# Query groups cut by batch: half tiles of one batch in a group, and all later query products in 32x32 tiles of one length

## The chip, the cores and the metric

The kernel runs on one core of a Trainium2 chip. The metric is the device time of one execution in microseconds (us). A measurement is the median over several executions, and smaller is better.

## What is computed

The reference takes q, k and v of 4 batches, 4 heads, 1088 positions and 32 numbers a head, and two 8x32 sketch matrices S1 and S2. It has an attention part and a feed-forward part:

```
phi(x) = outer product of S1 x and S2 x        (8 x 8 = 64 features for each position)
kv     = sum over positions of phi(k) v^T      (64 x 32 for each batch and head)
z      = sum over positions of phi(k)          (64 for each batch and head)
x      = phi(q) kv / (phi(q) z + 1e-6)         (4352 tokens of 4 heads x 32 = 128)
out    = elu(x w_in) w_out                     (128 -> 2048 -> 128)
```

All arithmetic in the kernel is fp32. Most of the work is the feed-forward part.

## The kernel before

**Half tiles, groups, units.** The 1088 positions of a batch are cut into NT = 17 half tiles of 64 positions, t = 0 to 16; four batches have 68. A group is eight half tiles, 512 tokens; groups 0 to 7 are full, and group 8, the last, has four half tiles. `half_tile(g, k)` (L498) says which batch and which t the k-th half tile of group g is. Before the change it counts straight through, so groups 2, 4 and 6 begin with the last half tiles of one batch (1, 2 and 3 of them) and go on with the next batch. For the query products, groups 4 and 5 are one unit, and so are 6 and 7; groups 2, 3 and 8 are units of their own (`units`, L545; `un[g]` is half the count of half tiles, so 4 for groups 2 and 3, 8 for the pairs and 2 for the last).

**Steps.** The feed-forward part goes through the 2048 hidden columns in eight slices `cp` of 256. One step is one group and one slice. For each step TensorE makes h = x w_in into two PSUM banks (`mm1`, L257), ScalarE and VectorE make elu of it (`e` at L867 and L869, `gg` at L875), and two steps later TensorE multiplies by w_out: as `o` (`mm2`, L257) for group 0, as `pb` (L768) for the first slices of group 1, and by seven products into `pa` and `pb` (L792) for the rest. The latter need sums `tt` of `gg` that GpSimd makes (L751 to L756). The list `steps` writes out the order by hand: 64 steps, the first ones alternating between groups 0 and 1, later ones group by group. The four half tiles of the last group follow in a tail of their own.

**The order of the rest.** All engines run their instructions in the order of the program. What belongs to the attention part is hung by hand on steps: `at(n, f)` puts f after the h products of step n, `mid` after the first half of elu, `late` after the second half.

**Keys.** For batches 1 to 3, `KF_late`, `KO`, `KA`, `Z`, `KV` make the features of the keys, kv and z. `KV_out` (L462) copies kv out of PSUM. It writes `kvs[b]`, one 32x32 block for each head, for 32x32 products, and `kvq[b]`, which has two heads in a block of 64 with zeros elsewhere (a VectorE multiplication by `cmask`), for 64x64 products. In the same way `Z_share` (L452) writes `SWq`, the sketches and z of two heads apart, and `SWs`, their sum over the two, the weights for 32x32 products.

**Queries.** `queries(g5, g1, n+1)` (L704) is hung on steps 13, 15, 22, 30, 46 and 62. It issues the products q5 of unit g5 (features of q times kv, L686; two halves f, which accumulate) and the products q1 of unit g1 (sketches of q and the denominator, L576). At step 13 there is only q1 of unit 2, at 15 q5 of 2 and q1 of 3, at 22 q5 of 3 and q1 of 4, at 30 q5 of 4 and q1 of 6, at 46 q5 of 6 and q1 of 8, at 62 only q5 of 8.

Units 2, 3 and 8 are `wide_tiles`: their products are 64x64 tiles of the array (four tiles) and write two banks of the pool `aux`. Units 4 and 6 use 32x32 tiles (sixteen tiles) and write four banks, two of `aux` and two of the pool `h`. Those two are the banks of the next step's h, taken early. That pool has four banks, two for each of two steps running.

Each tile of the array has its own run of half tiles. Where that run crosses from one batch to the next, `parts` (L558) splits it, and the product is made in pieces. All first pieces are issued, then the second ones (the sort by `j` at L572 and L681).

After the products VectorE transposes q1's result out of PSUM (`q1_out`, L589, tile `abw`), makes the denominator, its reciprocal and the features (`q2_den`, `q2_half`) and transposes these (`q4`, tile `qpT`). ScalarE copies q5's result into `xg`, the input of the h products (`q5_out`, L699 and L701).

The tile `qT[b]` has the transposed queries of one batch; batches 0 and 2 share one, and so do 1 and 3. Batch 2 is written over batch 0 at step 21, batch 3 over batch 1 late in step 24.

Of the kernel before, what the change touches and what calls it, by code (L numbers as in the profile page):

```python
# [27 lines left out]
def kernel(  # L28
# [44 lines left out]
    qT = [const.tile([FD, NT, 64], F32, name=f"qT{b}") for b in range(2)] * 2  # L73

# [168 lines left out]
    cmask = const.tile([P, 2], F32, name="cmask")  # L243
    nc.gpsimd.tensor_add(cmask[:], bmask[:, :2], bmask[:, 2:])
# [52 lines left out]
    SWq = const.tile([FD, B, 2, 4, R], F32, name="SWq")  # L297
    SWs = const.tile([FD, B - 1, 4, R], F32, name="SWs")
# [16 lines left out]
    def make_SWq():  # L315
        nc.gpsimd.memset(SWq[:, :, :, 3, :].rearrange("p b c r -> p (b c) r"), 0.0)
        for b in range(B):
            nc.gpsimd.tensor_copy(SWq[:, b, :, :2, :].rearrange("p c x r -> p x c r"), Sxp[:])
# [10 lines left out]
    kvq = {b: const.tile([P, 2, H, D], F32, name=f"kvq{b}") for b in (0, 1, 3)}  # L329
    kvs = {b: const.tile([P, 2, H, D], F32, name=f"kvs{b}") for b in (1, 2, 3)}  # L330
# [121 lines left out]
    def Z_share(b):  # L452
        z = wzs.pop(b)
        nc.gpsimd.tensor_add(SWq[:, b, :, 2, :], z[:, :2], z[:, 2:])
        if b:
            nc.gpsimd.tensor_add(SWs[:, b - 1], SWq[:, b, 0], SWq[:, b, 1])
# [5 lines left out]
    def KV_out(b, ps):  # L462
        if b in kvs:
            copy = nc.scalar.copy if b in kvq else nc.vector.tensor_copy
            copy(kvs[b][:].rearrange("p f h d -> p (f h d)"), ps[:, 128:384])
        if b in kvq:
            nc.vector.tensor_mul(kvq[b][:].rearrange("p f (g c) d -> p (f g) c d", c=2),
                                 ps[:, 128:384].rearrange("p (x c d) -> p x c d", c=2, d=D),
                                 _ap(cmask[:], [[0, 4], [1, 2], [0, D]]))
# [27 lines left out]

    def half_tile(g, k):  # L498
        return divmod(8 * g + k, NT)

    def runs(g):

        h = 0
        while h < 2 * qn[g]:
            b, t = divmod(8 * g + h, NT)
            m = min(2 * qn[g] - h, NT - t)
            yield b, t, h, m
            h += m
# [38 lines left out]

    def wide_tiles(g):
        return un[g] < 8

    def parts(g, w):  # L558

        n = un[g] if wide_tiles(g) else un[g] // 2  # L560
        k = 0
        while k < n:
            b, t = half_tile(g, n * w + k)
            m = min(n - k, NT - t)
            yield b, t, k, m
            k += m

    def q1(g, ps, o, opened):
        s = 64 if wide_tiles(g) else 32
        n = P // s  # L570
        todo = [(j, w, r, x) for w in range(n) for r in range(n) for j, x in enumerate(parts(g, w))]
        for j, w, r, (b, t, k, m) in sorted(todo, key=lambda x: x[0]):  # L572
            rows = slice(s * r, s * r + s)
            lhs = SWq[rows, b].rearrange("p c x r -> p (c x r)") if s > 32 else \
                SWs[rows, b - 1].rearrange("p x r -> p (x r)")
            nc.tensor.matmul(ps[r][s * w:s * w + s, o + 64 * k:o + 64 * (k + m)], lhs,  # L576
                             qT[b][rows, t:t + m, :].rearrange("p t s -> p (t s)"),
                             start=j == 0 and not any(ps[r] is x for x in opened), stop=True,
                             skip_group_check=True, tile_position=(s * r, s * w))
        abw[g] = ps, o  # L580
# [95 lines left out]
    def q5(g, ps, f):  # L676
        s = 64 if wide_tiles(g) else 32
        n = P // s
        m4 = H * un[g] // n
        todo = [(j, w, r, x) for r in range(n) for w in range(n) for j, x in enumerate(parts(g, w))]  # L680
        for j, w, r, (b, t, k, m) in sorted(todo, key=lambda x: x[0]):  # L681
            i, o = divmod(m4 * r, heads(g) * un[g])
            rows = slice(s * w, s * w + s)
            lhs = kvq[b][rows, f, 2 * r:2 * r + 2, :].rearrange("p c d -> p (c d)") if s > 32 else \
                kvs[b][rows, f, r, :]
            nc.tensor.matmul(ps[w][s * r:s * r + s, 64 * k:64 * (k + m)], lhs,  # L686
                             qpT[g, i][rows, o + 2 * k:o + 2 * (k + m), f, :],
                             start=(f == 0 and j == 0), stop=(f == 1),
                             skip_group_check=True, tile_position=(s * w, s * r))
        xps[g] = ps  # L690

    def q5_out(g, i=0):

        ps = xps[g]
        n = H * un[g] * 32 // len(ps)
        x = xg[g + i] = work.tile([P, 512], F32, name="xg", tag="xg", bufs=3)
        for w in range(2):
            if g < NQ - 1:
                nc.scalar.copy(x[:, n * w:n * w + n], ps[2 * i + w][:, :n])  # L699
            else:  # L700
                nc.scalar.copy(x[:, :2 * n].rearrange("p (k w s) -> p w k s", w=2, s=64)[:, w],  # L701
                               ps[w][:, :n].rearrange("p (k s) -> p k s", s=64))

    def queries(g5, g1, n):  # L704

        banks = lambda g: 0 if g is None else 2 if wide_tiles(g) else 4
        if banks(g5) + banks(g1) > 4:
            hs[steps[n]] = [psum.tile([P, 512], F32, name="h", tag="h", bufs=4) for c in range(2)]
        aux = [psum.tile([P, 512], F32, name="qps", tag="aux") for _ in range(2)]
        ps = {2: aux, 4: hs.get(steps[n], []) + aux}  # L710
        same = banks(g5) == banks(g1)
        if g5 is not None:
            q5(g5, ps[banks(g5)], 0)
            if not same:
                q5(g5, ps[banks(g5)], 1)
        if g1 is not None:
            q1(g1, ps[banks(g1)], 256 if g5 is not None else 0, ps[banks(g5)] if g5 is not None else [])
        if g5 is not None and same:
            q5(g5, ps[banks(g5)], 1)
# [100 lines left out]
    def fin_seven_b(g):  # L820
# [13 lines left out]
        for u in range(2):  # L834
            k = 0
            while k < 4:
                bt, t = half_tile(g, 4 * u + k)
                m = min(4 - k, NT - t)
                for lo in range(2):
                    r = slice(64 * u + 32 * lo, 64 * u + 32 * lo + 32)  # L840
                    for hi in range(2):
                        for w in range(2):
                            nc.sync.dma_start(rows[bt, w, hi, lo, :, t:t + m, :], ob[r, hi, k:k + m, w, :])
                k += m
# [46 lines left out]
    def fin1(g):  # L891
# [6 lines left out]
        for b, t, h, m in runs(g):  # L898
            for w in range(2):
                for q_ in range(4):  # L900
                    nc.sync.dma_start(rows[b, w, q_, :, t:t + m, :], oh[32 * q_:32 * q_ + 32, h:h + m, w, :])
# [301 lines left out]
```

## Time and profile before

| what | value |
|---|---|
| median of 3 runs | 265.75 us (265.56 to 265.98) |
| span of the profiled execution, first to last instruction | 263.3 us |
| what lies around the span, if that execution took the median | 2.45 us |
| TensorE busy | 257.8 us, 4127 matmul records |
| VectorE, ScalarE, GpSimd busy | 188.2, 184.5, 168.2 us |
| clock granted to TensorE | 1.000 |

The profile is of one execution, which has no time of its own in the table other than its span. Lines L... are lines of the kernel before. Every fp32 matmul leaves two records, and so does every load of weights (PEld). In a timeline row the columns are start, time from the first start to the last end, engine, line, operation, tiles, array tile or shape, and count of records; a bracket names the idle time before the row and what ended it. Times of one engine's rows overlap by the depth of its pipeline, so starts are better compared than ends.

### The profile page before, as it was taken

Reading aid. Unit: us, or ns where it says so; the run is one execution under the profiler, and the core shown is the slowest. Engines: PE = TensorE matmul, PEld = TensorE weight load, DVE = VectorE, ACT = ScalarE, POOL = GpSimd, SP = SyncE. Lnnn points to the kernel's source line nnn. Section 1 sums busy time; section 2 is a strip of 40 time slices with the busy share of each in tenths; the row PEclk is TensorE's granted clock in tenths of the full one; section 3 lists DMA queues with packets and bytes.
Section 4 is the critical chain, followed back from the end, with each engine's and each line's share of the span. In section 5 each row is a group of like instructions: output and inputs, shape, how many; then the busy total and the mean of one; then the engine's idle time right before and its main releaser. Section 6 shows DMA issues by size and latency. Waiting matters only on the chain.

```text
span 263.3 us, 9739 instructions
## 1 busy us (share of the span) xinstructions
PE 257.8 (98%) x4127; PEld 160.5 (61%) x4127; DVE 188.2 (71%) x349; ACT 184.5 (70%) x356; POOL 168.2 (64%) x251
## 2 busy tenths in 40 slices
PE   8899999999999999999999999999999999999994
PEld 7652334354346756667666666665666666667994
DVE  6899999997969997996477676644446445674651
ACT  2479978677567656775587777776777777777793
POOL 4400009105477996798869799888688888998300
PEclk9999999999999999999999999999999999999999
DMA  5997099020011110000100110011001100110011
GB/s 176 339 349 209 2 277 230 1 72 18 2 24 26 26 20 2 2 4 17 31 3 0 29 18 0 2 19 25 3 2 21 23 4 0 18 20 8 2 30 32
DMA packets 26442, 13.73 MB, mean 52 GB/s; under 512 B 19328, under 2 KB 24576, under 8 KB 26400
## 3 DMA queue, kind: packets, MB, share of 16 engines
q1 hardware_dynamic: 25968, 12.76, 18.9%
q8 instruction: 32, 0.52, 0.9%
q10 hardware_dynamic: 368, 0.30, 0.3%
q0 software_dynamic: 64, 0.07, 0.1%
q14 instruction: 10, 0.08, 0.1%
HBM read 10.88 MB, written 2.23 MB: 50 GB/s over the span
## 4 chain that ended last, share of the span: by engine, by line
PE 96%; POOL 1%; DVE 1%; ACT 1%; issue 0%
PE h L257 44%; PE pb L792 16%; PE pa L792 13%; PE o L257 5%; PE pb L768 4%; PE ol L257 3%; PE idle L265 1%; PE kv L428 1%; PE h L686 1%; PE qps L686 1%; POOL kp L324 1%; PE kfps L360 1%; PE qps L576 1%; PE qtp L636 1%; PE kv L257 1%; PE abp L341 1%
## 5 line engine op out<-in xcount | busy, mean ns | idle before, releaser
L257 PE MATMUL h<-xg,W 128*32 128x512 f32 (+3 forms) x904 | 130.7, 539 | 0.4 <-ACT xg L649 0.4
L875 DVE SCALAR_TENSOR_TENSOR gg<-e,h 128x512 f32<-128x512 f32 x128 | 85.6, 683 | 54.1 <-ACT e L869 50.6
L867 ACT ACTIVATE e<-h 128x512 f32<-128x512 f32 x128 | 75.5, 590 | 45.6 <-PE h L257 42.9
L869 ACT ACTIVATE e<-e 128x512 f32<-128x512 f32 x128 | 80.9, 632 | 3.8
L257 PEld LDWEIGHTS h<-xg,W 128*32 128x32 f32 (+1 forms) x904 | 42.6, 122 | 43.2 <-issue 34.9
L754 POOL TENSOR_TENSOR tt<-gg 128x256 f32<-128x256 f32 x50 | 37.0, 741 | 16.4 <-DVE gg L875 16.1
L751 POOL TENSOR_TENSOR tt<-gg 128x256 f32<-128x256 f32 x50 | 36.7, 734 | 5.5 <-DVE gg L875 5.1
L755 POOL TENSOR_TENSOR tt<-tt,gg 128x256 f32<-128x256 f32 x50 | 37.5, 750 | 3.9
L756 POOL TENSOR_TENSOR tt<-gg,tt 128x256 f32<-128x256 f32 x50 | 37.2, 744 | 3.9
L792 PEld LDWEIGHTS pa<-gg,W 128*64 128x64 f32 (+1 forms) x496 | 23.8, 125 | 23.5 <-issue 22.9
L792 PE MATMUL pa<-gg,W 128*64 128x128 f32 (+1 forms) x496 | 30.5, 274 | 0.0
L792 PE MATMUL pb<-tt,SS 128*64 128x128 f32 (+1 forms) x480 | 29.5, 273 | 0.0
L792 PEld LDWEIGHTS pb<-tt,SS 128*64 128x64 f32 (+1 forms) x480 | 22.6, 126 | 0.0
L792 PE MATMUL pa<-tt,SS 128*32 128x128 f32 (+1 forms) x288 | 21.0, 273 | 0.0
L133 POOL TENSOR_TENSOR raw<-raw,tiny 128x512 f32<-128x512 f32 x1 | 1.0, 1044 | 29.4 <-DVE raw L128 29.4
L792 PE MATMUL pb<-tt,W 128*64 128x128 f32 (+1 forms) x256 | 19.8, 273 | 0.0
L792 PE MATMUL pb<-gg,SS 128*64 128x128 f32 (+1 forms) x256 | 19.8, 273 | 0.0
L257 PE MATMUL o<-gg,W 128*32 128x512 f32 x128 | 15.3, 594 | 0.0
L792 PEld LDWEIGHTS pa<-tt,SS 128*32 128x32 f32 (+1 forms) x288 | 13.6, 124 | 0.0
L792 PEld LDWEIGHTS pb<-gg,SS 128*64 128x64 f32 (+1 forms) x256 | 12.7, 125 | 0.0
L792 PEld LDWEIGHTS pb<-tt,W 128*64 128x64 f32 (+1 forms) x256 | 12.6, 125 | 0.0
L768 PE MATMUL pb<-gg,W 128*32 128x256 f32 x192 | 11.5, 380 | 0.0
(163 smaller groups left out, 279.5 us busy)
## 6 DMA issues: line engine op xcount, KB each, us to landing
raw<-in_moe_w_in_dram SPq DMA_DIRECT2D x8, 256.0 KB, 6.6
raw<-in_moe_w_out_dram SPq DMA_DIRECT2D x8, 256.0 KB, 6.4
hd_k<-in_k_dram SPq DMA_DIRECT2D x3, 544.0 KB, 7.3
hd_q<-in_q_dram SPq DMA_DIRECT2D x3, 544.0 KB, 7.9
out_dram<-ob SPq DMA_DIRECT2D x88, 16.0 KB, 1.5
v<-in_v_dram SPq DMA_DIRECT2D x4, 288.0 KB, 6.8
v<-in_v_dram SPq DMA_DIRECT2D x4, 256.0 KB, 8.3
hd_k<-in_k_dram SPq DMA_DIRECT2D x1, 288.0 KB, 3.3
```

The lines of the kernel that those rows point to most:

```text
L257: nc.tensor.matmul(dst[c:c + tile], lhs[:, c:c + tile], rhs, skip_group_check=True, tile_position=(0, c), **kw)
L265: nc.tensor.matmul(idle[c:c + tile, :cols], ones[:, :tile], ones[:, :cols], skip_group_check=True, tile_position=(0, c))
L686: nc.tensor.matmul(ps[w][s * r:s * r + s, 64 * k:64 * (k + m)], lhs, qpT[g, i][rows, o + 2 * k:o + 2 * (k + m), f, :], start=(f == 0 and j ...
L751: nc.gpsimd.tensor_tensor(t[:, 0], b12, b11, op=SUB)
L754: nc.gpsimd.tensor_tensor(t[:, 2], b22, b12, op=SUB)
L755: nc.gpsimd.tensor_tensor(t[:, 1], t[:, 2], b11, op=ADD)
L756: nc.gpsimd.tensor_tensor(t[:, 3], b21, t[:, 1], op=SUB)
L768: nc.tensor.matmul(acc[1][0][r:r + width[0], 256 * hi:256 * hi + 256], lhs[:, w:w + width[0]], gg[:, c, 256 * u:256 * u + 256], start=(cp ...
L792: nc.tensor.matmul(bank[r:r + width[0], P * col:P * col + P], lhs[:, w:w + width[0]], rhs[:, u], start=(first and i in ((0,) if g == 1 els ...
L867: nc.scalar.activation(e, hs[g, cp][c][:, :n], RELU, scale=-1.0)
L869: nc.scalar.activation(e, e, EXP, scale=-1.0)
L875: nc.vector.scalar_tensor_tensor(gs[g, cp][:, c, :n], es[g, cp][:, c, :n], -1.0, hs[g, cp][c][:, :n], op0=ADD, op1=MAX)
```

## The change

Groups now hold half tiles of one batch: group g has the half tiles 8(g mod 2) to 8(g mod 2)+7 of batch g//2, and the last group has half tile 16 of each batch. `parts` and `runs` are gone, since nothing crosses a batch; `quarter_of` gives each of the four row or column strips of the array one run of n half tiles of one batch.

All units from 2 on use 32x32 tiles and four banks, so `queries` always takes the two h banks of the next step, and always in the order q5 first half, q1, q5 second half. `kvq`, `SWq` and `cmask` are gone; `kvs` and `SWs` exist for all batches, `SWs` made by GpSimd in `make_SWs` and `Z_share`. `q1_out` and `q5_out` empty four banks instead of two for units 2, 3 and 8, each operation half as wide. `qE` keeps half tile 16 of batches 0 and 1, copied by GpSimd at steps 3 and 14 (`keep_last`), because `qT` is written over before the last group needs it. The output transfers of groups 2, 4 and 6 are no longer split at a batch (24 fewer).

```diff
+    qE = const.tile([FD, 2, 64], F32, name="qE")
...
-    def make_SWq():
-        nc.gpsimd.memset(SWq[:, :, :, 3, :].rearrange("p b c r -> p (b c) r"), 0.0)
+    def make_SWs():
+        nc.gpsimd.memset(SWs[:, :, 3, :], 0.0)
         for b in range(B):
-            nc.gpsimd.tensor_copy(SWq[:, b, :, :2, :].rearrange("p c x r -> p x c r"), Sxp[:])
+            nc.gpsimd.tensor_add(SWs[:, b, :2, :], Sxp[:, :, 0, :], Sxp[:, :, 1, :])
...
     def Z_share(b):
         z = wzs.pop(b)
-        nc.gpsimd.tensor_add(SWq[:, b, :, 2, :], z[:, :2], z[:, 2:])
-        if b:
-            nc.gpsimd.tensor_add(SWs[:, b - 1], SWq[:, b, 0], SWq[:, b, 1])
+        zh = work.tile([FD, 2, R], F32, name="zh", tag="zh")
+        nc.gpsimd.tensor_add(zh[:], z[:, :2], z[:, 2:])
+        nc.gpsimd.tensor_add(SWs[:, b, 2, :], zh[:, 0], zh[:, 1])
...
     def KV_out(b, ps):
-        if b in kvs:
-            copy = nc.scalar.copy if b in kvq else nc.vector.tensor_copy
-            copy(kvs[b][:].rearrange("p f h d -> p (f h d)"), ps[:, 128:384])
-        if b in kvq:
-            nc.vector.tensor_mul(kvq[b][:].rearrange("p f (g c) d -> p (f g) c d", c=2),
-                                 ps[:, 128:384].rearrange("p (x c d) -> p x c d", c=2, d=D),
-                                 _ap(cmask[:], [[0, 4], [1, 2], [0, D]]))
+        copy = nc.scalar.copy if b % 2 else nc.vector.tensor_copy
+        copy(kvs[b][:].rearrange("p f h d -> p (f h d)"), ps[:, 128:384])
...
+    def keep_last(b):
+        nc.gpsimd.tensor_copy(qE[:, b, :], qT[b][:, NT - 1, :])
+
     def half_tile(g, k):
-        return divmod(8 * g + k, NT)
+        return (g // 2, 8 * (g % 2) + k) if g < NQ - 1 else (k, NT - 1)
...
+    def quarter_of(g, w):
+        n = un[g] // 2
+        return (*half_tile(g + n * w // 8, n * w % 8), n)

     def q1(g, ps, o, opened):
-        s = 64 if wide_tiles(g) else 32
-        n = P // s
-        todo = [(j, w, r, x) for w in range(n) for r in range(n) for j, x in enumerate(parts(g, w))]
...
+        for w in range(4):
+            b, t, n = quarter_of(g, w)
+            qs = qE[:, b:b + 1, :] if g == NQ - 1 and b < 2 else qT[b][:, t:t + n, :]
+            for r in range(4):
+                rows = slice(32 * r, 32 * r + 32)
+                nc.tensor.matmul(ps[r][32 * w:32 * w + 32, o:o + 64 * n], SWs[rows, b].rearrange("p x r -> p (x r)"),
+                                 qs[rows].rearrange("p t s -> p (t s)"),
+                                 start=not opened, stop=True, skip_group_check=True, tile_position=(32 * r, 32 * w))
...
     def q5(g, ps, f):
...
+        m4 = un[g]
+        for r in range(4):
             i, o = divmod(m4 * r, heads(g) * un[g])
...
+            for w in range(4):
+                b, t, n = quarter_of(g, w)
+                rows = slice(32 * w, 32 * w + 32)
+                nc.tensor.matmul(ps[w][32 * r:32 * r + 32, :64 * n], kvs[b][rows, f, r, :],
+                                 qpT[g, i][rows, o:o + 2 * n, f, :], start=(f == 0), stop=(f == 1),
+                                 skip_group_check=True, tile_position=(32 * w, 32 * r))
...
     def q5_out(g, i=0):
-        ps = xps[g]
-        n = H * un[g] * 32 // len(ps)
+        n = 32 * un[g]
+        ps = xps[g] if len(units[g]) == 1 else xps[g][2 * i:2 * i + 2]
...
+        for w in range(len(ps)):
+            nc.scalar.copy(x[:, n * w:n * w + n], ps[w][:, :n])

     def queries(g5, g1, n):
-        banks = lambda g: 0 if g is None else 2 if wide_tiles(g) else 4
-        if banks(g5) + banks(g1) > 4:
-            hs[steps[n]] = [psum.tile([P, 512], F32, name="h", tag="h", bufs=4) for c in range(2)]
-        aux = [psum.tile([P, 512], F32, name="qps", tag="aux") for _ in range(2)]
-        ps = {2: aux, 4: hs.get(steps[n], []) + aux}
-        same = banks(g5) == banks(g1)
+        hs[steps[n]] = [psum.tile([P, 512], F32, name="h", tag="h", bufs=4) for c in range(2)]
+        ps = hs[steps[n]] + [psum.tile([P, 512], F32, name="qps", tag="aux") for _ in range(2)]
         if g5 is not None:
-            q5(g5, ps[banks(g5)], 0)
-            if not same:
-                q5(g5, ps[banks(g5)], 1)
+            q5(g5, ps, 0)
         if g1 is not None:
-            q1(g1, ps[banks(g1)], 256 if g5 is not None else 0, ps[banks(g5)] if g5 is not None else [])
-        if g5 is not None and same:
-            q5(g5, ps[banks(g5)], 1)
+            q1(g1, ps, 256 if g5 is not None else 0, g5 is not None)
+        if g5 is not None:
+            q5(g5, ps, 1)
...
-            b, t = half_tile(NQ - 1, u * qn[NQ - 1] + i)
+            b, t = half_tile(NQ - 1, 2 * i + u)
...
     late(2, make_Sxp)
-    late(2, make_SWq)
+    late(3, keep_last, 0)
+    late(14, keep_last, 1)
+    late(2, make_SWs)
```

More of the change, by code (lines that the diff above doesn't have):

```diff
@@ L240 @@
                             ident[:].rearrange("p (x j) -> p x j", j=R), axis=AX, op=ADD)
-    cmask = const.tile([P, 2], F32, name="cmask")
-    nc.gpsimd.tensor_add(cmask[:], bmask[:, :2], bmask[:, 2:])
     hmask = const.tile([P, H], F32, name="hmask")
@@ L296 @@
     SW = const.tile([FD, H, 3, R], F32, name="SW")
-    SWq = const.tile([FD, B, 2, 4, R], F32, name="SWq")
-    SWs = const.tile([FD, B - 1, 4, R], F32, name="SWs")
+    SWs = const.tile([FD, B, 4, R], F32, name="SWs")
     keep_warm(3)
@@ L328 @@
     kvS = const.tile([P, H, D], F32, name="kvS")
-    kvq = {b: const.tile([P, 2, H, D], F32, name=f"kvq{b}") for b in (0, 1, 3)}
-    kvs = {b: const.tile([P, 2, H, D], F32, name=f"kvs{b}") for b in (1, 2, 3)}
+    kvs = {b: const.tile([P, 2, H, D], F32, name=f"kvs{b}") for b in range(B)}
     kv_ps, kvz, feats, wzs, kf_ps = {}, {}, {}, {}, []
@@ L496 @@
         nc.gpsimd.memset(pw[:, :, R:], 1e-6)
+    def keep_last(b):
+        nc.gpsimd.tensor_copy(qE[:, b, :], qT[b][:, NT - 1, :])
     def half_tile(g, k):
-        return divmod(8 * g + k, NT)
[L501 to L508, printed above, removed]
+        return (g // 2, 8 * (g % 2) + k) if g < NQ - 1 else (k, NT - 1)
     def q1_first():
@@ L546 @@
     un = {g: sum(qn[x] for x in gr) for g, gr in units.items()}
[L555 to L566, printed above, removed]
-    def q1(g, ps, o, opened):
-        s = 64 if wide_tiles(g) else 32
-        n = P // s
-        todo = [(j, w, r, x) for w in range(n) for r in range(n) for j, x in enumerate(parts(g, w))]
[L572 to L579, printed above, removed]
+    def quarter_of(g, w):
+        n = un[g] // 2
+        return (*half_tile(g + n * w // 8, n * w % 8), n)
+    def q1(g, ps, o, opened):
+        for w in range(4):
[6 more added lines that the diff above has]
+                                 start=not opened, stop=True, skip_group_check=True, tile_position=(32 * r, 32 * w))
         abw[g] = ps, o
@@ L676, in q5 @@
     def q5(g, ps, f):
[L677 to L681, printed above, removed]
-            i, o = divmod(m4 * r, heads(g) * un[g])
[L683 to L689, printed above, removed]
+        m4 = un[g]
@@ L692, in q5_out @@
     def q5_out(g, i=0):
-        ps = xps[g]
-        n = H * un[g] * 32 // len(ps)
+        n = 32 * un[g]
+        ps = xps[g] if len(units[g]) == 1 else xps[g][2 * i:2 * i + 2]
         x = xg[g + i] = work.tile([P, 512], F32, name="xg", tag="xg", bufs=3)
[L697 to L702, printed above, removed]
@@ L834, in fin_seven_b @@
         for u in range(2):
[L835 to L844, printed above, removed]
+            bt, t = half_tile(g, 4 * u)
+            for lo in range(2):
+                r = slice(64 * u + 32 * lo, 64 * u + 32 * lo + 32)
+                for hi in range(2):
+                    for w in range(2):
+                        nc.sync.dma_start(rows[bt, w, hi, lo, :, t:t + 4, :], ob[r, hi, :, w, :])
     def mm1(g, cp, cs=(0, 1)):
@@ L897, in fin1 @@
         oh = ob[:].rearrange("p i u w d -> p (i u) w d")
[L898 to L901, printed above, removed]
+        b, t = half_tile(g, 0)
+        for w in range(2):
+            for q_ in range(4):
+                nc.sync.dma_start(rows[b, w, q_, :, t:t + 8, :], oh[32 * q_:32 * q_ + 32, :, w, :])
     last = [(i, cp) for i in range(2) for cp in range(NP)]
```

## The prediction

> **What bounds the kernel now.** I read the busy times and the chain that ended last on the page first, then TensorE's timeline around the six places where query products run, then VectorE's timeline ahead of the second of them.
>
> ```profile
> PE 257.8 (98%) x4127; PEld 160.5 (61%) x4127; DVE 188.2 (71%) x349; ACT 184.5 (70%) x356; POOL 168.2 (64%) x251
> PE 96%; POOL 1%; DVE 1%; ACT 1%; issue 0%
> ```
>
> The chain is TensorE for 96% of the span, so time taken out of TensorE's queue comes off the end unless another engine is late there. A full product h takes 1.72 us from start to next start (67.70 to 69.42 below). The query products are the rows L576 (q1) and L686 (q5).
>
> ```profile
> 61.77 1.94 PE L257 MATMUL h<-xg,W 128*32 128x512 f32 x16
> 63.64 0.66 PE L576 MATMUL qps<-qT,SWq 64*64 64x64 f32 x12
> 64.23 1.93 PE L768 MATMUL pb<-gg,W 128*32 128x256 f32 x32
> ...
> 67.70 1.90 PE L257 MATMUL o<-gg,W 128*32 128x512 f32 x16
> 69.42 1.90 PE L257 MATMUL h<-xg,W 128*32 128x512 f32 x16
> 71.25 0.67 PE L686 MATMUL qps<-qpT,kvq 64*64 64x64 f32 x12
> ...
> 72.72 1.92 PE L257 MATMUL o<-gg,W 128*32 128x512 f32 x16
> ```
>
> Columns: start, time, engine, line, operation, tile, count of records (each fp32 matmul leaves two). From the first query record to the next full product, the six stretches take 0.59 us (step 13: 63.64 to 64.23), 1.47 (step 15: 71.25 to 72.72), 1.94 (step 22: 99.03 to 100.97), 2.40 (step 30: 128.77 to 131.17), 1.97 (step 46: 183.24 to 185.21) and 0.60 (step 62: 237.28 to 237.88): 8.97 us. About 0.1 us of idle ahead of each (71.25 against 69.42+1.72) stays, since the tile shape still changes there. TensorE meets no queue but its own, so these 8.97 us are what the change can touch.
>
> What a 32x32 product costs, and what a split piece costs:
>
> ```profile
> 100.17 0.30 PE L576 MATMUL h<-qT,SWs 32*32 32x128 f32 x2
> ...
> 100.27 0.41 PE L576 MATMUL qps<-qT,SWs 32*32 32x256 f32 x2
> 100.31 0.27 PE L576 MATMUL h<-qT,SWs 32*32 32x128 f32 x2
> ...
> 100.44 0.38 PE L576 MATMUL h<-qT,SWs 32*32 32x256 f32 x2
> ...
> 100.97 0.64 PE L792 MATMUL pa<-gg,W 128*32 128x128 f32 x16
> ```
>
> Sixteen 32x32 products start within 0.107 us (6.7 ns apart) when they come after a change of shape. A tile's second pass starts 0.24 us after its first for 256 columns and 0.133 for 128, where the stream alone is 0.216 and 0.108 (the steady start-to-start of 256-column passes in the 64x64 stretch is 0.216). So one product holds its tile 0.456 us at 256 columns, 0.24 at 128 and, by the same step, about 0.13 at 64.
>
> ```profile
> 183.61 0.73 PE L686 MATMUL h<-qpT,kvs 32*32 32x64 f32 x8
> ...
> 184.03 0.41 PE L686 MATMUL qps<-qpT,kvs 32*32 32x256 f32 x2
> 184.06 0.41 PE L686 MATMUL h<-qpT,kvs 32*32 32x192 f32 x2
> 184.09 0.41 PE L686 MATMUL qps<-qpT,kvs 32*32 32x256 f32 x2
> ...
> 184.83 0.45 PE L576 MATMUL qps<-qT,SWq 64*64 64x128 f32 x8
> ```
>
> Two things are seen. The four leftover 64-column pieces all fall on one row of tiles and stretch from 183.61 to past 183.9, while the other twelve tiles have nothing. And products that follow other 32x32 products start 16.7 ns apart (two to each of the last three rows, and these 0.033 us apart), not 6.7.
>
> **The change part by part.** The listing of both programs has 240 query matmuls after against 162 before, all 32x32, no leftover pieces, three passes in the order q5 first half, q1, q5 second half. I lay them out with 6.7 ns starts for the first sixteen, 16.7 ns for the rest, the tile times above and 0.09 us to the next full product (at step 22 the last pass starts at 100.77, streams 0.108, and the next product starts at 100.97).
> - Step 13, 16 of 128 columns: 0.107+0.24+0.09 = 0.44; gain 0.15.
> - Step 15, 48 of 128: last group starts 0.25 after the last start of the second, which is 0.24+0.25; 0.24+0.25+0.017+0.25+0.24+0.09 = 1.09; gain 0.38.
> - Step 22, 16 of 128, 16 of 256, 16 of 128: 0.24+0.456+0.25+0.24+0.09 = 1.28, and 0.10 for a wait that stays (the second 64x64 record waits there from 99.03 to 99.154 for the bank that VectorE leaves at 99.10): 1.38; gain 0.56. The change of shape between q5(3) and q1(4), 0.09, is in this.
> - Step 30, 48 of 256: 3 x 0.456+0.25+0.09 = 1.71; gain 0.69.
> - Step 46, 16 of 256, 16 of 64, 16 of 256: 0.456+0.267+0.25+0.456+0.09 = 1.52; gain 0.45.
> - Step 62, 32 of 64: 0.107+0.267+0.14+0.09 = 0.60; gain 0.
> Sum 2.23 us. If all groups started 6.7 ns apart, each stretch would be the sum of its tile times and 0.10+0.09 (and the 0.10 of step 22): 0.44, 0.91, 1.23, 1.56, 1.23 and 0.45, gain 3.15. That is the other end; the steady rows are at 16.7, so I stay near the first.
>
> The change also adds a wait. Steps 13, 15 and 62 (and q5 at 22) now write two banks of the pool h, which the step before must have left: its second gg on VectorE must be done.
>
> ```profile
> 69.28 1.24 DVE L673 STREAM_TRANSPOSE qpT<-qp 128x1024 f32<-128x1024 f32 x1
> 70.45 0.65 DVE L875 SCALAR_TENSOR_TENSOR gg<-e,h 128x512 f32<-128x512 f32 x1
> 71.02 1.29 DVE L281 STREAM_TRANSPOSE kT<-hd_k 128x1088 f32<-128x1088 f32 x1
> ```
>
> At step 15 that gg ends at 71.10, after a VectorE chain without a gap since 64.20, and four 128x128 transposes stand in that chain where two of 128x256 did. The two took 0.70 us start to start; 128x128 ones at step 46 took 0.32 and 0.27, 0.24 and 0.20 without the overlap, so four take 0.84: +0.14. The bank is free at 71.24, seen by TensorE 0.05 later (99.10 to 99.154), while TensorE is ready at 71.25-0.15 = 71.10: a new wait of 0.19. Behind it in TensorE's queue stand q1(3), the second half of q5(2) and the o product, all of which end later by it. At step 13 the gg before ends at 62.11 against 63.64, at step 62 at 236.42 against 237.28: nothing.
>
> Afterwards the next h product must wait until copies and transposes leave its two banks. The hardest place is step 30, already so before: transposes end at 132.46, h starts at 132.74. Elsewhere the operations are half as wide; ScalarE has about 0.1 us more (four copies of 128x128: the two at step 62 start 0.16 apart; two of 128x256 take 0.53) and stands idle 1.1 and 1.6 us before them at steps 15 and 22; at step 62 it has 0.2, but the sums made of that step are read 2.1 us after they are ready, 242.75 to 244.89. I take nothing.
>
> Costed at nothing: three VectorE multiplications for kvq (0.42 us each) go and one copy (0.41) comes, in a queue that then waits 1.1 us for ScalarE at step 13; GpSimd gets two copies of 128x64 (a 128x32 copy takes 0.21), one in a 1.25 us hole at 74.2, and its sums are ready 1.2 us or more before TensorE reads them at the tightest step (t3 of step 23 ends at 110.84, read at 112.04), so a step that came 1.2 us closer would show it; 24 output transfers fewer leave SP's queue, which nothing waits for. The end of the kernel has the same instructions.
>
> Sum: 2.23-0.19 = 2.04 us; 3.15-0.19 = 2.96 at the other end. I take 2.15. The profiled execution has a span of 263.3 us, 2.45 below the median of 265.75; I keep that rest, so 265.75-2.15 = 263.6, with a span near 261.15.
>
> Two rules of the Trainium skill speak against it. ScalarE's and VectorE's evacuation above leaves room; the page "TensorEngine Tiling (Array Packing)", Performance Considerations, warns that tiling speeds up TensorE but not the emptying of PSUM, which may become the limit. If that held at the three narrow stretches, the extra 0.11 and 0.14 us would come back there, 0.75 in all, and the time would be 264.35; the sum does not use it. The same section gives each matmul about 60 cycles of overhead; 78 more of them, one after another, would by an estimate from that page's figure (60 cycles at the 2.4 GHz of the page "TensorE: Matmul & The Clock Gate", What's actually happening) give back 1.95 us, 265.55; the sixteen starts within 0.107 us above speak against their being paid one after another.
>
> **The rivals.**
> (a) Slower: a 32x32 product costs what it costs in step 30 now, 2.40-0.09 us for 60, 38.5 ns each, because it is the count and not the split that is paid. Then 240 x 38.5 = 9.24, plus 0.19 wait, plus 6 x 0.09 to the next product, is 9.97 against 8.97: 266.75. It decides above 34 ns per product. For it: no unsplit run of three groups is in the trace. Against: the 16.7 ns starts, and the 0.73 us row of leftovers that explains the mean.
> (b) The other engines eat part: VectorE's chain from 84.5 to 99.10 does not move up with TensorE, so that the 0.34 won by step 15 is waited away at step 22, and the 0.11+0.14 of emptying shows ahead of h after steps 22 and 62, 0.50: 2.04-0.84 = 1.20, 264.55. Against: at 76.86 that chain waits for ScalarE, which waits for TensorE, and h has the room shown above.
> (c) All starts 6.7 ns apart: 262.8.
> (d) Nothing: the gains are refilled by waits for banks, 265.5 to 266.
>
> **How the numbers follow.** Forecast 0.68, (c) 0.12, (b) 0.10, (d) 0.04, (a) 0.06. The range goes from just under (c), 262.7, to (b), 264.6; outside it are (d), (a) and part of the tails. A measurement can tell about 0.2%, 0.53 us, from no change. Forecast, (b) and (c) are beyond it: faster 0.90, same 0.04, slower 0.06.
>
> **What would show it.** The six stretches should read 0.44, 1.09, 1.38, 1.71, 1.52 and 0.60 us; the first q5 record of step 15 should lie 0.05 us later than now and be preceded by a VectorE gg; h after step 30 should follow pb without a gap. A mean over 34 ns per 32x32 product, or new idle time ahead of h after steps 13, 15, 22 or 62, would make the forecast wrong.

## The result, and the profile after

The changed kernel takes 264.75 us (median of 6 runs, 264.62 to 264.81) beside 265.76 us for the kernel before (6 runs, 265.39 to 265.98): a ratio of 0.9967, 95% interval 0.9955 to 0.9978, or 1.01 us. Timed again later, beside other runs of the kernel before (experiment e9 below), it is 264.73 us against 265.50: 0.9972 (0.9962 to 0.9982), 0.77 us. So the change is faster, as forecast, but by a third to a half of the 2.15 us that were forecast, and the time lies above the range given.

The page says at once that the bound has not changed:

```profile
PE 257.2 (98%) x4283; PEld 160.2 (61%) x4283; DVE 188.0 (72%) x353; ACT 184.8 (70%) x362; POOL 169.7 (65%) x253
PE 95%; DMA 1%; DVE 1%; ACT 0%; issue 0%; SPq 0%; DVEq 0%
```

TensorE has 156 records more (78 matmuls of two) and is busy 0.6 us less; it is still 95% of the chain that ended last. The 1% of DMA in that chain is the load of the first keys in the opening, before any of the steps that the change touches. How long the opening takes is no effect of the change: TensorE reaches step 13 at 63.64 us in the profile before, at 63.88 and 63.65 in the two of the changed kernel (the second is e9 below), and between 63.59 and 64.02 in its variants.

TensorE's timeline around steps 13 and 15 (columns as before: start, time, engine, line, tile, shape, count of records):

```profile
62.01 1.94 PE L256 MATMUL h<-xg,W 128*32 128x512 f32 x16
63.88 0.30 PE L545 MATMUL h<-qT,SWs 32*32 32x128 f32 x2
...
64.32 1.94 PE L722 MATMUL pb<-gg,W 128*32 128x256 f32 x32
...
69.50 1.91 PE L256 MATMUL h<-xg,W 128*32 128x512 f32 x16
71.34 0.30 PE L651 MATMUL h<-qpT,kvs 32*32 32x128 f32 x2
...
71.58 0.28 PE L651 MATMUL qps<-qpT,kvs 32*32 32x128 f32 x2
71.66 0.41 PE L545 MATMUL h<-qT,SWs 32*32 32x128 f32 x3
71.79 0.31 PE L545 MATMUL qps<-qT,SWs 32*32 32x128 f32 x2
...
72.54 0.28 PE L651 MATMUL qps<-qpT,kvs 32*32 32x128 f32 x2
72.75 1.06 PE L256 MATMUL o<-gg,W 128*32 128x512 f32 x8
```

Step 13 takes 0.44 us, exactly as forecast. Step 15 takes 1.41 and not 1.09: the first sixteen products are issued as dense as at step 13, one more (q1's first) starts at 71.66, and the next only at 71.79. The six stretches together:

| step | before | forecast | after | difference from before |
|---|---|---|---|---|
| 13 | 0.59 | 0.44 | 0.44 | -0.15 |
| 15 | 1.47 | 1.09 | 1.41 | -0.06 |
| 22 | 1.94 | 1.38 | 1.70 | -0.24 |
| 30 | 2.40 | 1.71 | 2.06 | -0.34 |
| 46 | 1.97 | 1.52 | 1.74 | -0.23 |
| 62 | 0.60 | 0.60 | 0.79 | +0.19 |
| sum | 8.97 | 6.74 | 8.14 | -0.83 |

The step that shows why is step 30, where all 48 products have 256 columns:

```profile
128.57 0.41 PE L651 MATMUL h<-qpT,kvs 32*32 32x256 f32 x2
...
128.81 0.39 PE L651 MATMUL h<-qpT,kvs 32*32 32x256 f32 x2
...
129.03 0.59 PE L545 MATMUL h<-qT,SWs 32*32 32x256 f32 x2
129.24 0.40 PE L545 MATMUL qps<-qT,SWs 32*32 32x256 f32 x1
...
129.87 0.41 PE L651 MATMUL qps<-qpT,kvs 32*32 32x256 f32 x2
...
130.30 0.39 PE L651 MATMUL qps<-qpT,kvs 32*32 32x256 f32 x2
130.62 0.66 PE L746 MATMUL pa<-gg,W 128*64 128x128 f32 x8
```

The first rows (128.57 on) are the first passes of sixteen products, those from 128.81 their second passes. The seventeenth starts at 129.03, which is when its tile is free (128.57 and the forecast's 0.456). The eighteenth does not start at 129.05, as the forecast has it, but at 129.22. It is the second record of the 0.59 us row: in the single records its weights load at 129.215 and it starts at 129.219. No semaphore is recorded at that load, and its tile is free; what has just happened is that the first product's second pass has ended, at 129.184 (the row of 128.81 joins two records). The next such gap ends with the thirty-fifth product, at 129.87: seventeen products and 0.65 us on, where the forecast has 0.456 for sixteen. From this comes theory W below.

Step 62, 32 products of 64 columns, is the one that lost:

```profile
236.50 0.24 PE L651 MATMUL h<-qpT,kvs 32*32 32x64 f32 x2
...
236.68 0.22 PE L651 MATMUL qps<-qpT,kvs 32*32 32x64 f32 x2
236.77 0.30 PE L651 MATMUL h<-qpT,kvs 32*32 32x64 f32 x3
236.85 0.25 PE L651 MATMUL qps<-qpT,kvs 32*32 32x64 f32 x2
...
237.13 0.23 PE L651 MATMUL qps<-qpT,kvs 32*32 32x64 f32 x2
237.29 0.66 PE L746 MATMUL pa<-gg,W 128*64 128x128 f32 x8
```

After sixteen dense starts the seventeenth starts at 236.77 and the eighteenth at 236.83 (the third record of that row), 0.33 us after the first, although a 64-column product streams only twice 0.054.

Last, VectorE ahead of step 15, where a new wait of 0.19 us had been forecast:

```profile
69.48 1.24 DVE L641 STREAM_TRANSPOSE qpT<-qp 128x1024 f32<-128x1024 f32 x1
70.64 0.65 DVE L825 SCALAR_TENSOR_TENSOR gg<-e,h 128x512 f32<-128x512 f32 x1
71.21 1.29 DVE L280 STREAM_TRANSPOSE kT<-hd_k 128x1088 f32<-128x1088 f32 x1
```

The gg ends at 71.29 and q5 starts at 71.34, 0.52 us after the last h record, as the first query product of step 13 does (63.35 to 63.88). There is no wait, though no slack either.

### The profile page after: what moved, and what is told of

Read it like the earlier page. It is cut to its first block, busy times and chain, and to the rows that moved or that the text cites. A ratio compares the mean times of both kernels' runs of the same rounds, so it can differ in the third digit from the quotient of the medians.

```text
span 262.8 us, 10041 instructions
## 1 busy us (share of the span) xinstructions
PE 257.2 (98%) x4283; PEld 160.2 (61%) x4283; DVE 188.0 (72%) x353; ACT 184.8 (70%) x362; POOL 169.7 (65%) x253
## 4 chain that ended last, share of the span: by engine, by line
PE 95%; DMA 1%; DVE 1%; ACT 0%; issue 0%; SPq 0%; DVEq 0%
PE h L256 45%; PE pb L746 16%; PE pa L746 13%; PE o L256 5%; PE pb L722 4%; PE ol L256 3%; DMA hd_k<-in_k_dram 1%; PE kv L425 1%; PE h L651 1%; PE h L545 1%; PE abp L338 1%; PE qps L651 1%; PE kfps L357 1%; PE qtp L604 1%; PE kv L256 1%; DVE qp L592 0%
```

## The experiments

Three theories stand in the expectations. **T** is the forecast's layout: a tile takes the next group's product as soon as it is free. **R** makes the choice and order of the tiles decide, by the loading of weights or the emptying of PSUM that neighbours share. **W**, the window, is read from the start times above: TensorE has only 17 of these products under way, and product n+17 loads its weights some 0.03 us after product n is complete, about 0.16 us after its last column was streamed. (The profile models the ends of products, so the split into 0.16 and 0.03 is the profile's; the distances between starts are measured.) From a product to the seventeenth behind it, W has two passes and 0.217 us, however many columns: 0.325 us at 64, 0.433 at 128, 0.649 at 256. The expectations charge this to each group of sixteen. By W's own count, and in the traces, it is seventeen; what this does to the sums is said at e8.

**e1, q1 three times.** The products q1 of steps 13, 30 and 46 are issued three times over, with the same result.

```diff
             q1(g1, ps, 256 if g5 is not None else 0, g5 is not None)
+            if n - 1 in (13, 30, 46):
+                for _ in range(2):
+                    q1(g1, ps, 256 if g5 is not None else 0, g5 is not None)
```

> The changed kernel with the sixteen q1 products issued three times instead of once at steps 13 (128 columns), 30 (256) and 46 (64); the sums it makes are three times too large in numerator and denominator alike. Theory W, formed from the trace of the changed kernel: TensorE holds 17 fp32 products at a time, the weights of product n+17 load about 0.03 us after product n has completed, so that a group of sixteen behind another costs two passes and 0.22 us: 0.433 us at 128 columns, 0.649 at 256, 0.325 at 64. Stretches from the first query record to the next full product: step 13 0.44+0.87 = 1.31, step 30 2.06+1.30 = 3.36, step 46 1.74+0.65 = 2.39. The prediction's layout T (a tile goes on as soon as it is free, starts 16.7 ns apart): step 13 0.44+0.52 = 0.96, step 30 2.06+0.91 = 2.97, step 46 1.74+0.53 = 2.27. Rival R (a row of tiles takes the next weights 0.10 us after its last pass has ended) gives the same as W here.

Measured: 1.416 us at step 13, 3.321 at 30, 2.360 at 46, where W's sums had 1.31, 3.36 and 2.39; steps 15, 22 and 62 as in the changed kernel (1.416, 1.723, 0.785). Step 13 with three times sixteen products of 128 columns takes what step 15 takes, 48 products of 128 columns with other weights, other data and two kinds of products. So it is neither the wait for VectorE nor the change between q5 and q1 that stretches step 15. The added groups cost 0.488 us each at step 13, 0.632 at 30 and 0.311 at 46, within 0.06 of W's 0.433, 0.649 and 0.325, where T has 0.26, 0.456 and 0.27.

**e2, rows first.** Both loops over tiles swapped, so that four neighbours in issue order share a row of the array where they shared a column.

```diff
-        for r in range(4):
-            i, o = divmod(m4 * r, heads(g) * un[g])
-            for w in range(4):
+        for w in range(4):
+            for r in range(4):
+                i, o = divmod(m4 * r, heads(g) * un[g])
```

> The changed kernel with the order of the sixteen products turned: the four of one row of tiles come one after another, then the next row; before, the row changed with every product. Theory W (17 products at a time): the six stretches stay as they are within 0.04 us: 0.44, 1.42, 1.71, 2.06, 1.74, 0.79. Rival R (a row of tiles waits for the end of its own last pass): the first row's last start is about 0.02 after its first, not 0.09, so each passage from a group to the next is 0.07 shorter: 0.44, 1.28, 1.57, 1.92, 1.60, 0.72.

Measured: 0.440, 1.415, 1.630, 2.055, 1.735 and 0.784 us. Five stretches are those of the changed kernel within 0.005 us, so the order of the tiles does not set the pace. The page "TensorE: Matmul & The Clock Gate" of the Trainium skill, Part 3, says that weights load beside a running matmul only when the row group differs, and in the same part lets loads into a background weight buffer go ahead too. The first of these alone does not hold here: in step 30 of the changed kernel all 32 weight loads of the first sixteen products start from 128.57 to 128.70 us, while first passes stream in all four rows of tiles until 128.78 at the earliest; and the swap of the order changes nothing. Step 22 gets 0.075 us shorter for another reason: in this order the first four products go to one bank, and the bank that VectorE leaves last is needed later. In e9, an execution of the unswapped kernel in which TensorE came later to step 22, that stretch is 1.630 as well.

**e3, eight tiles at a time.** The left eight tiles do all three passes, then the right eight.

```diff
+        for cols in (range(2), range(2, 4)):
...
-            q5(g5, ps, 0)
+                q5(g5, ps, 0, cols)
...
-            q1(g1, ps, 256 if g5 is not None else 0, g5 is not None)
+                q1(g1, ps, 256 if g5 is not None else 0, g5 is not None, cols)
...
-            q5(g5, ps, 1)
+                q5(g5, ps, 1, cols)
```

> The changed kernel with the three passes done for the left eight tiles and then for the right eight, the same products in all. A tile meets its next product after eight others, so never more than 17 are under way for long and the tile itself is the limit (0.243 us for 128 columns, 0.459 for 256, about 0.13 for 64). Theory W: step 13 unchanged 0.44; step 15 6 x 0.243+0.14 = 1.60; step 22 2.15; step 30 6 x 0.459+0.14 = 2.89; step 46 2.24; step 62 0.66 to 0.79. Rival R or any emptying of the array between groups (0.22 over the two passes for each of six groups, a little less with eight products): step 15 about 2.4, step 30 about 3.8, step 46 about 3.1, step 62 about 1.3.

Measured: 0.440, 1.519, 2.026, 2.587, 2.055 and 0.784 us. With eight tiles the tiles themselves become the limit, and the stretches grow by 0.10, 0.32, 0.53 and 0.32 us: under W's sum, which took the halves one after the other, and far under R's. Half the tiles cost only 7% to 26%, so in the changed kernel the sixteen tiles are not the limit. R is out, in its form of neighbours that hold each other up as well.

**e4, grouping alone.** Groups of one batch (with `qE`), but units 2, 3 and 8 stay in 64x64 tiles with `kvq` and `SWq`. The edit in short, against the kernel before:

```diff
+    WIDE, GROUPED = (2, 3, 8), True
...
     def half_tile(g, k):
-        return divmod(8 * g + k, NT)
+        g, k = g + k // 8, k % 8
+        if not GROUPED:
+            return divmod(8 * g + k, NT)
+        return (g // 2, 8 * (g % 2) + k) if g < NQ - 1 else (k, NT - 1)
...
     def wide_tiles(g):
-        return un[g] < 8
+        return g in WIDE
```

> One part of the change alone: groups of one batch, but units 2, 3 and 8 stay in 64x64 tiles and two banks as before; units 4 and 6 lose their leftover pieces, the last unit's two strips are in two pieces of 64 columns. Theory W: step 13 four products of 256 columns, 4 x 0.108+0.14 = 0.57 (0.59 before); step 15 twelve, 1.30+0.14 = 1.44 (1.47); step 22 1.94-0.2 for the leftover pieces = 1.75; step 30 2.06; step 46 q5(6) two groups and q1(8) in 64x64, 1.30+0.10+0.09+0.30 = 1.79; step 62 0.60. Sum 8.2 against 8.97 before: 0.75 us faster, 265.0 beside 265.75. The prediction's layout T had 0.69 at step 30 and 0.45 at step 46 from the leftover pieces, 0.2 at step 22: over 1.3 us faster, 264.4.

Measured: 265.12 us against 265.51 (0.9984, 0.9975 to 0.9993); stretches 0.593, 1.456, 1.821, 2.059, 1.819 and 0.626, 0.59 less than before (W had 0.75, T over 1.3). But 0.32 us comes back on TensorE at step 20, in the products `kfps`. VectorE's timeline there, of the changed kernel and then of this one:

```profile
94.46 0.41 DVE L461 COPY kvs<-kv 128x256 f32<-128x256 f32 x1
94.79 1.23 DVE L641 STREAM_TRANSPOSE qpT<-qp 128x1024 f32<-128x1024 f32 x1
```

```profile
94.36 0.41 DVE L476 COPY kvs<-kv 128x256 f32<-128x256 f32 x1
94.69 0.41 DVE L478 TENSOR_TENSOR kvq<-kv,cmask 128x256 f32<-128x256 f32 x1
95.03 1.23 DVE L692 STREAM_TRANSPOSE qpT<-qp 128x1024 f32<-128x1024 f32 x1
```

And TensorE's, in the same order:

```profile
95.03 0.72 PE L357 MATMUL kfps<-kT,Sxp 64*32 64x288 f32 x16
```

```profile
94.93 1.03 PE L367 MATMUL kfps<-kT,Sxp 64*32 64x288 f32 x16
```

In this grouping the last unit has a half tile of every batch, so a 64x64 unit 8 needs `kvq` for batch 2 too, which neither kernel has. That is one multiplication more in a VectorE queue without a gap, which moves what follows by 0.33 us and keeps the bank `kv` that much longer; `kfps` takes 0.31 us longer. In e11 below, which makes `kvq` elsewhere, the 0.32 us is gone.

**e5, narrow tiles alone.** The groups of before, with their pieces, and all units in 32x32 tiles; in short, against the kernel before:

```diff
+    WIDE, GROUPED = (), False
...
     def wide_tiles(g):
-        return un[g] < 8
+        return g in WIDE
```

> The other part alone: groups run across batches as before, with split pieces, but units 2, 3 and 8 use 32x32 tiles and four banks. Theory W: step 13 20 products, 0.44+0.16 = 0.60; step 15 56 products, 1.42 and about 0.2 for each of three split groups less a little, 1.8; step 22 as before for q1(4), about 1.9; steps 30 and 46 as before, 2.40 and 1.9; step 62 0.79. Sum about 9.4 against 8.97: slower by 0.3 to 0.5 us, 266.1. Layout T: step 62 0.60, step 15 1.4, 22 1.6: faster by 0.4, 265.3.

Measured: 266.17 us against 265.51 (1.0026, 1.0017 to 1.0035): slower. Stretches 0.584, 1.584, 1.780, 2.397, 1.904 and 0.784, +0.06 us in all. The profiled execution has TensorE standing still for 0.5 us in the middle of step 22's products `pb` as well (see the last section), and its opening is 0.2 us late. How much of the 0.66 us these are in the other ten runs is open. What is certain from the stretches: without the grouping, narrow tiles bring nothing; the pieces that cross a batch make it 276 products, for 240 in the changed kernel.

**e6 and e7, one unit or two left wide.** In e6 only unit 8, in e7 units 2 and 3 keep 64x64 tiles; groups as in the changed kernel. Against e4, first e6 and then e7 (in each, `kvq`, `kvs` and `SWs` are made for the batches that need them):

```diff
-    WIDE, GROUPED = (2, 3, 8), True
+    WIDE, GROUPED = (8,), True
```

```diff
-    WIDE, GROUPED = (2, 3, 8), True
+    WIDE, GROUPED = (2, 3), True
```

> The changed kernel with only the last unit back in 64x64 tiles and two banks, two pieces of 64 columns to a strip. Theory W: step 62 has 16 products of 64x64, 4 to a tile at 0.108, 0.43+0.14 = 0.60 instead of 0.79; step 46 loses 0.06 by the change of shape. Together 0.1 to 0.15 us faster than the changed kernel: 264.62. Layout T: no difference at step 62, 0.1 slower at 46.

> The changed kernel with units 2 and 3 back in 64x64 tiles and two banks, now without leftover pieces; the last unit stays in 32x32. Theory W: step 13 0.57 (0.44 in 32x32), step 15 1.44 (1.42), step 22 1.75 (1.71), the rest as in the changed kernel: 0.15 to 0.2 us slower than the changed kernel, 264.9. Layout T had 32x32 at 0.44, 1.09 and 1.38 there: 0.85 slower.

Measured: e6 264.90 us against 265.51 (0.9976, 0.9966 to 0.9986), stretches 0.440, 1.414, 1.732, 2.055, 1.818 and 0.625. Step 62 is back at 0.63 (16 products for 32), step 46 at 1.82 and step 22 at 1.73, 0.05 us gained in all, and the 0.32 us of `kvq` for batch 2 is there as in e4. e7 264.77 us (0.9967, 0.9956 to 0.9979), stretches 0.592, 1.456, 1.829, 2.056, 1.735 and 0.784: 0.31 us longer than the changed kernel's in the profile (W had 0.15 to 0.2; step 22 took 1.83 for its 1.75), not to be told from it in time. Unsplit 64x64 units cost nearly what the narrow ones do: 1.456 against 1.415 at step 15.

**e8, each long product as two.** Every 256-column product becomes two of 128, the second sixteen after the first, so columns, data and tiles stay and only the number of products grows. The loop of q5 (that of q1 likewise):

```diff
-        for r in range(4):
-            i, o = divmod(m4 * r, heads(g) * un[g])
+        for j, r in [(j, r) for j in range(un[g] // 4 or 1) for r in range(4)]:
+            i, o = divmod(m4 * r, heads(g) * un[g])
...
+                n = n // (un[g] // 4 or 1)
+                oj, c = o + 2 * n * j, 64 * n * j
```

> Every 256-column product of units 4 and 6 is done as two products of 128 columns, the second sixteen after the first, so the columns streamed and the data are those of the changed kernel and only the number of products grows: step 22 from 48 to 64 products, step 30 from 48 to 96, step 46 from 48 to 80. Theory W (sixteen products cost two passes and 0.217 us, whatever came before): each added group of sixteen costs 0.217 us more, so step 22 goes from 1.705 to 1.92 us, step 30 from 2.057 to 2.71, step 46 from 1.737 to 2.17; sum +1.30 us, steps 13, 15 and 62 unchanged. The forecast's own layout (a tile goes on as soon as it is free, starts 16.7 ns apart) would give 6 x 0.267+0.44 = 2.04 at step 30, no more than the measured 2.06, so no change. Count of products at 38.5 ns each (the slower rival): 64, 96 and 80 products are 2.55, 3.79 and 3.17 us.

Measured: 0.441, 1.416, 1.910, 2.670, 2.145 and 0.785 us, against W's 1.92, 2.71 and 2.17 at the three steps that changed. TensorE's timeline at step 30, 96 products; the rows from 130.73 on are the first after a gap:

```profile
129.85 0.30 PE L655 MATMUL h<-qpT,kvs 32*32 32x128 f32 x2
...
130.17 0.41 PE L655 MATMUL h<-qpT,kvs 32*32 32x128 f32 x3
...
130.73 0.31 PE L547 MATMUL qps<-qT,SWs 32*32 32x128 f32 x2
...
131.15 0.30 PE L547 MATMUL qps<-qT,SWs 32*32 32x128 f32 x2
...
131.59 0.30 PE L655 MATMUL h<-qpT,kvs 32*32 32x128 f32 x2
...
132.02 0.30 PE L655 MATMUL h<-qpT,kvs 32*32 32x128 f32 x2
...
132.53 0.33 PE L750 MATMUL pa<-gg,W 128*64 128x128 f32 x2
```

In the single records the eighteenth product starts 0.437 us after the first (the third record of the row of 130.17), and after it every seventeenth, the 35th, 52nd, 69th and 86th, at 0.871, 1.305, 1.740 and 2.175: 0.434 us for seventeen products, without drift. This is the clearest run: T has 2.04, the price of 38.5 ns for each product 3.79.

Counted by seventeens, W also gives whole stretches: so many full windows, 16.7 ns for each start after that, the last product's second pass and stream, and 0.09 us. For step 15 (48 = 2 x 17+14) this is 2 x 0.434+13 x 0.0167+0.133+0.108+0.09 = 1.416 us, for e8's step 30 (96 = 5 x 17+11) 5 x 0.434+10 x 0.0167+0.133+0.108+0.09 = 2.668, and for the changed kernel's step 30, with 0.648 for a window of 256 columns, 2 x 0.648+13 x 0.0167+0.24+0.216+0.09 = 2.059. Measured are 1.415, 2.670 and 2.057; e1's step 13 has the 48 products of step 15 and the same 1.416. These sums were made after the runs.

Here 48 more products for the same columns cost 0.613 us, 12.8 ns each, which is W's 0.217 us shared by seventeen. By the Trainium skill ("TensorEngine Tiling (Array Packing)", Performance Considerations) each matmul has about 60 cycles of overhead, which at the 2.4 GHz of the page "TensorE: Matmul & The Clock Gate", What's actually happening, would be an estimated 25 ns; the price measured here, with many tiles under way at once, is half of it.

**e9, the changed kernel again; e10, rows first, timed; e11, a version from what was learned.** e11 has rows first and unit 8 wide, with `kvq` made late, from the copies in SBUF (the last of these edits, against e6):

```diff
     def KV_out(b, ps):
...
-        if b in kvq:
-            nc.vector.tensor_mul(kvq[b][:].rearrange("p f (g c) d -> p (f g) c d", c=2),
-                                 ps[:, 128:384].rearrange("p (x c d) -> p x c d", c=2, d=D),
-                                 _ap(cmask[:], [[0, 4], [1, 2], [0, D]]))
+
+    def make_kvq(b):
+        nc.vector.tensor_mul(kvq[b][:].rearrange("p f (g c) d -> p (f g) c d", c=2),
+                             kvs[b][:].rearrange("p f (g c) d -> p (f g) c d", c=2),
+                             _ap(cmask[:], [[0, 4], [1, 2], [0, D]]))
...
+    for b in range(B):
+        late(50 + 2 * b, make_kvq, b)
```

> The changed kernel itself, on the chip and beside the runs of the kernel before that the next two kernels share. If TensorE's six stretches (0.83 us shorter together in the profile) are the whole of the gain, the median lies 0.8 us under the kernel before; the 1.01 us of the first comparison would then hold 0.2 us that comes from elsewhere.

> The changed kernel with both loops over tiles in the order rows first, timed. Theory W: one profile of it gave step 22 at 1.630 us for 1.705 because the first four products there do not need the bank that VectorE leaves last, and all else alike, so 0.08 us under the changed kernel, hardly above what the comparison can tell. If order mattered to the weight loads, it would be more than 0.3 us either way.

> Rows first for the 32x32 units, and the last unit's two halves in 64x64 tiles again (8 products for 16, of two columns' weights), its masked copies of the four K-V sums made by VectorE from the copies in SBUF at steps 50 to 56 and not from the bank at step 20. Theory W with what the kernels before it measured: step 22 1.63, step 46 1.82, step 62 0.63, so the six stretches are 0.08+0.16-0.08 = 0.16 us shorter than the changed kernel's, and the 0.32 us that the masked copy of batch 2 cost at step 20 is gone: 0.15 us under the changed kernel. If the four multiplications of 0.42 us delay VectorE at steps 50 to 56 where it has no room, up to 0.3 us each comes back.

Measured, all against 265.50 us (14 runs): e9 264.73 us (0.9972, 0.9962 to 0.9982), e10 264.51 (0.9966, 0.9953 to 0.9978), e11 264.68 (0.9972, 0.9960 to 0.9983). e9's 0.77 us (interval 0.48 to 1.01) agrees with the 0.83 us of the stretches, so no second source is needed for the gain. e11's stretches are 0.440, 1.414, 1.630, 2.055, 1.816 and 0.625, 0.16 us less than the changed kernel's, as expected, and nothing comes back at step 20: its four multiplications take 0.42 us each from 199.7 us on and delay nothing on TensorE. In time, neither e10 nor e11 can be told from the changed kernel; the intervals overlap almost wholly. No version here is shown to beat it.

## Why the prediction was wrong, point by point

**What held.** TensorE is the bound, and only the six stretches changed: along TensorE's queue, no other place between step 13 and the last product moves by more than about a hundredth of a microsecond from before to after. The 0.09 us to the first query product stayed. Step 13, one group of sixteen, came out at 0.44. What was costed at nothing cost nothing: h follows pb without a gap after step 30 (the last pb starts at 131.99, h at 132.20), and no new idle time stands ahead of h after steps 13, 15, 22 or 62. Neither of the two things that the forecast let eat into the gain, emptying and VectorE's chain (rival b), is seen.

**The step that failed** is "a tile starts the next group's product when it is free", with starts 16.7 ns apart. It gave each later group of sixteen 0.25 us at 128 columns, 0.456 at 256 and about 0.27 at 64. Measured, from a product to the seventeenth behind it, are 0.434 (e8's ladder), 0.648 (e1's step 30) and 0.325 (step 62). The difference is nearly the same at 128 and 256 columns, 0.19 us: the time from a product's last column until the one seventeen places on loads its weights. e3 shows that it is not the tile that takes this time: there, with eight tiles in turn, a tile takes its second product 0.243 us after its first at 128 columns (step 15) and 0.456 at 256 (step 30), as the forecast had it. The two rows on which the step stood were read rightly and taken too far. The 6.7 ns starts are those of the first sixteen after a change of shape, which fill an empty window. The 16.7 ns starts are those of a window being refilled, at a rate that says nothing of when the refill begins. In the row of step 46 that the prediction shows (183.61 to past 183.9, twelve tiles idle) the gap was put down to the four leftover pieces alone; taking these away at step 30 gained 0.34 us and not 0.69. The trace of before held the window already: at its step 30 too, where products are split, the eighteenth loads its weights 0.431 us after the first start.

**The forecast's terms.** Steps 15, 22, 30 and 46 were forecast to gain 0.38, 0.56, 0.69 and 0.45 and gained 0.06, 0.24, 0.34 and 0.23; step 62 was forecast at no change and lost 0.19, because its two groups have a window to wait for and 64x64 tiles, with half the products, fit into one. The forecast's other end, all groups 6.7 ns apart, was still farther off; both ends came from the one wrong picture, and the range between them held no case in which groups do not overlap. The prediction's sign of being wrong, over 34 ns for a 32x32 product, is met at step 30 (2.06-0.09 us for 48, 41 ns), though not by the mean of all 240 (32 ns).

**The wait at step 15**, 0.19 us, was not there: from step 13's first product to step 15's pass 7.46 us where 7.61 did, so the whole gain of step 13 is kept. Four transposes in the place of two took 0.83 us from start to start for 0.70, as forecast; but the multiplication `pw` behind them fell from 0.48 to 0.31 us, which the working had left at its old duration. From the gg after step 13 to the end of the one ahead of step 15 VectorE needed 6.85 us where it had needed 6.89.

**Span and time.** The prediction kept 2.45 us between span and time, from the median and one profiled execution that need not be the same. In every run that gives both, 1.7 to 2.0 us lie around the span, 1.82 for the changed kernel's profiled one (262.8 and 264.62). If that holds for the execution profiled before, it was some 0.6 us faster than its median. That the two spans differ by only 0.45 us is seen in the traces: the changed kernel's reaches step 13 0.23 us later, and from the start of its last TensorE record to the end it takes 3.81 us for 3.67, which leaves 0.45 of the 0.83.

**The rivals.** (a) named the right kind of cause, a price per product that the split does not explain, and was wrong in its size: it took one price for all lengths. Per product W has 19, 26 and 38 ns at 64, 128 and 256 columns once a window is full; (a) has 38.5 for all, too much below 256, so its 266.75 came out too slow. That it is right at 256 is luck, since it was the mean of a split mix of lengths. (b) came nearest in time, 264.55, by a mechanism that the runs do not show. (c) and T fall with the same step. (d) needed waits for banks, and only 0.075 us of such a wait is seen, at step 22, in the kernel before as after.

**Which half of the change brings the gain.** By the stretches, grouping alone is 0.59 us of the 0.83, narrow tiles on top of it 0.24, and narrow tiles without grouping -0.06. The timings agree in sign (0.39 us for e4 with its 0.32 us of `kvq`, -0.66 for e5).

## What to carry to other kernels

When independent products in small tiles are laid out by hand, do not cost a later group by the tile's own passes: look in the trace for the first product that starts late though its tile is free, and see which product ended just before. If a fixed number is under way at once, each batch of that number has a fixed cost, so fewer and longer products are worth more than more tiles, and a boundary that splits products costs time although no column is added. A dense burst at the start of a stretch only fills the window and is no rate.

## What the runs showed of the hardware

- **A window of 17 fp32 products in 32x32 tiles.** Product n+17 loads its weights about 0.03 us after product n is complete, itself some 0.16 us after its last column. From a product to the seventeenth behind it pass 0.434 us at 128 columns (five times in a row in e8), 0.648 at 256 (four times in e1) and 0.325 at 64 (step 62), whatever the order of the tiles (e2). That it is a count is inferred from start times, whose gaps come after every seventeenth product at all three lengths. What is counted is open: a product leaves two weight loads and two passes, so seventeen are 34 of each. Open too is why the seventeenth itself starts 0.08 us after its tile is free at 128 columns (0.32 for 0.24 us after the first start, step 15), which it does not at 256.
- **TensorE can stand still with no wait on record.** In e9, the changed kernel's second profile, fifteen of the sixteen records of narrow `pb` products stretch over 1.07 us, and for 0.41 us of it nothing starts; in e8 the same happens after step 22, for 0.96 us, and in e5 for 0.50. TensorE's timeline, of e9 and then of e8:

```profile
88.33 1.07 PE L746 MATMUL pb<-tt,SS 128*32 128x128 f32 x15
89.11 0.37 PE L746 MATMUL pa<-tt,SS 128*32 128x128 f32 x3
```

```profile
101.72 0.61 PE L750 MATMUL pb<-tt,SS 128*32 128x128 f32 x13
103.02 0.30 PE L750 MATMUL pb<-tt,SS 128*32 128x128 f32 x2 [0.69 <-issue]
```

The profile gives no releaser ("issue"), no semaphore is recorded at the product that ends the gap, and neither the profile of before nor the first one of after has such a gap. It comes and goes between executions of one kernel, so it may be part of why runs of the kernel before spread over 0.6 to 0.8 us; that was not tested, and its cause is open.
